# Gated linear attention with a mixer on one core: TensorE's small products in two groups a unit, with 48 weight columns for the later updates of the state

## The chip, the core and the metric

The kernel runs on one core of a Trainium2 chip. Its time is the device time of one execution in microseconds; the median of three runs is given. The core has a matrix engine (TensorE, PE in the profile, with its weight loads shown as PEld), a vector engine (VectorE, DVE), a scalar engine (ScalarE, ACT), GpSimd (POOL) and SyncE (SP), which here issues the transfers between memory and the core. Each engine works through its own queue in order, and they meet at semaphores.

## The reference

An attention with gates, in which each head keeps a 48 x 48 state that decays by a gate for every row, and then a mixer over the sequence and the channels:

```python
# q, k, v, f_logit: (4, 8, 768, 48)
f = 1.0 / (1.0 + np.exp(-f_logit))
for t in range(S):
    state = f[:, :, t, :, None] * state + einsum('bhd,bhe->bhde', k[:, :, t], v[:, :, t])
    y[:, :, t] = einsum('bhd,bhde->bhe', q[:, :, t], state)
x = y.transpose(0, 2, 1, 3).reshape(4, 768, 384)
# U: (768, 32), V: (32, 768), w_ch1: (384, 1536), w_ch2: (1536, 384)
u = x + (x.transpose(0, 2, 1) @ U @ V).transpose(0, 2, 1)
out = u + np.maximum(u @ w_ch1, 0.0) @ w_ch2
```

All arithmetic is in 32-bit floats.

## The kernel before

The attention is cut into 16 units, four for each batch; a unit is two heads of one batch. The two heads lie in the two halves of the 128 partitions, each padded from 48 to 64 rows (PAD). The 768 steps are cut into 12 chunks of 64. Within a chunk the products of gates are formed by scans on VectorE, the queries and keys are scaled by them, and what a chunk passes on is a 48 x 48 matrix.

A unit has a front, made by `prepare`, and a rear, made by `attend`. The front, mostly VectorE: `gates` (turn the gate logits, sigmoid on ScalarE), `keep` (backward scan L694), `keys` (turn and scale), `read_back` (forward scan L712), `queries` (turn and scale). Up to unit 5 the turning is done by TensorE's transposes (L660), later by VectorE (L637). The rear, mostly TensorE:

- `scores` (L788): keys times queries inside each chunk, 24 matmuls of 64 x 64, into the tile `sc`; VectorE masks it into `A` (L795).
- `kept` (L809): 12 transposes of the keys into `pt`, copied by ScalarE to `kb`.
- `states` (L825): `kb` times v, 24 matmuls into `ds`. The weights are 64 columns a head, of which 48 carry data. One ScalarE copy (L831) moves it to `added`.
- `scan` (L846): one VectorE scan runs the state through all chunks; after batch 0 ScalarE copies the result to `st` (L851).
- `read` (L863): queries times `st`, 22 matmuls that open the accumulation in `y`. A tiny ScalarE copy `seen` (L870) of one column follows.
- `inner` (L881): `A` times v, 24 matmuls that add to `y`; they wait for `seen`. ScalarE copies `y` to `x` (L887).

These matmuls fill only a quarter of TensorE's array each (64 rows by 64 columns; the key transposes half of it), and four of them can be in flight together. The matmuls of the mixer use the whole array: `pz` (L258, first layer, with a relu on ScalarE, L268), `po` (L283, second layer), `pw` (L312, second layer with seven products for eight), `pp` (L410, a scheme with fewer products for the last blocks), and the low-rank part (`ph`, `pu`, `put`).

The attention of a batch is interleaved with the mixer of the batch before. `steps(first, last)` yields the pieces of the attention, ten for a unit in the middle of a range; `attention` calls `Fill` before each piece, which hands out that much of the mixer's big products as falls to one piece. TensorE's order is the order in which the pieces are called. VectorE's and ScalarE's orders are also taken as called up to the attention of batch 1; later a scheduler sets them by priority. In step n, `steps` calls:

```python
for n in range(first, last):
    yield from rear(n - 1, "scores") + rear(n, "kept") + front(n + 1, "gates", "keep", "keys")
    yield from rear(n - 1, "read")
    made = rear(n, "states", "scan")
    yield lambda: [f() for f in made]
    yield from front(n + 1, "read_back", "queries") + rear(n - 1, "inner")
    if n + 2 < NU:
        load(n + 2, "v")
```

So big products can fall between any two of these. The outputs of all matmuls lie in PSUM: `ps_big` has three tiles of two banks for the small products, the transposes and some others, `ps_mm` two of one bank for `pz`, `po` and `pw`. v lies in three buffers, loaded by `load`.

Of the kernel before, what the change touches and what calls it, by code (L numbers as in the profile page):

```python
# [21 lines left out]
PAD = 64  # L22
# [450 lines left out]
def factored_path(ctx, tc, q, k, v, f_logit, moe_U, moe_V, moe_w_ch1, moe_w_ch2, out, ok):  # L473
# [4 lines left out]
    nc = tc.nc  # L478
    B, H, S, D = q.shape
    P = nc.NUM_PARTITIONS  # L480
# [3 lines left out]
    NBL = S // P  # L484
# [6 lines left out]
    NU = B * HP  # L491
# [36 lines left out]
    v_tiles = {}  # L528

    def load(n, *names):  # L530

        b, hp = divmod(n, HP)
        for nm in names:
            if nm == "v":
                v_tiles[n] = three.tile([P, NBL, 2, D], F32, name="v_nat")
            for par in range(2):
                head = src[nm][b, 2 * hp + par]
                if nm == "v" and par:

                    for s in range(2):  # L540
                        nc.sync.dma_start(
                            out=v_tiles[n][(1 - s) * C : (2 - s) * C, :, par, :],
                            in_=head.rearrange("(c s p) d -> s p c d", s=2, p=C)[s],
                        )
                    continue
                if nm == "v" or n < TURNED:
                    dst = v_tiles[n] if nm == "v" else nat[n % 2][nm]
                    nc.sync.dma_start(out=dst[:, :, par, 0:D], in_=head.rearrange("(c p) d -> p c d", p=P))
                    continue
                head = head.rearrange("(c i) d -> i c d", i=NB)  # L550
                for part in range(2):
                    p0 = par * PAD + part * NB
                    n_ch = min(NB, D - part * NB)
                    nc.sync.dma_start(  # L554
                        out=raw[n % 2][nm][p0 : p0 + NB, :].rearrange("p (c d) -> p c d", d=NB)[:, :, 0:n_ch],
                        in_=head[:, :, part * NB : part * NB + n_ch],
                    )
# [38 lines left out]
    added = const.tile([P, D * NCH + 1], F32, name="added")  # L596
# [173 lines left out]
    def attend(n):  # L770

        b, hp = divmod(n, HP)
        T = units[n]
        vt = v_tiles[n]
        rows = [slice(par * PAD, par * PAD + D) for par in range(2)]
        chunk = [slice(c * C, (c + 1) * C) for c in range(NCH)]

        part = [slice(s * C, (s + 1) * C) for s in range(2)]
# [37 lines left out]

        def states():

            ds = ps_big.tile([P, 2, 512], F32, name="ds", tag="big")
            for c in range(NBL):  # L820
                for s in range(2):
                    for par in range(2):

                        i = (c + (s & par)) % NBL
                        nc.tensor.matmul(  # L825
                            ds[par * PAD : (par + 1) * PAD, s, c * D : (c + 1) * D],
                            lhsT=T["kb"][part[s ^ par], par, i, :], rhs=vt[part[s ^ par], c, par, :],
                            start=True, stop=True,
                        )

            nc.scalar.copy(  # L831
                added[:, 1:].rearrange("p (e c s) -> p e c s", c=NBL, s=2),
                ds[:, :, 0 : NBL * D].rearrange("p s (c e) -> p e c s", e=D),
            )

        def scan():

            st = T["st"] = two.tile([P, NCH, D], F32, name="st")
            by_e = "p (e c) -> p c e"
            if b == 0:  # L840
                states = st.rearrange("p c e -> p (c e)")
                T["st"] = states.rearrange(by_e, c=NCH)
            else:
                states = added[:, 0 : D * NCH]
            with tc.high_priority(offset=AHEAD):
                nc.vector.tensor_tensor_scan(  # L846
                    states, added[:, 0 : D * NCH], T["whole"].rearrange("p e c -> p (e c)"), 0.0, ALU.add, ALU.mult
                )
                if b > 0:

                    nc.scalar.copy(st, states.rearrange(by_e, c=NCH))  # L851
# [20 lines left out]
        def inner():  # L872
# [18 lines left out]
            del units[n], v_tiles[n]  # L891

        return [kept, states, scan, scores, read, inner]

    ahead, here = {}, {}

    def front(n, *names):

        if n >= NU:
            return []  # L900
        if n not in ahead:
            ahead[n] = dict(zip(("gates", "keep", "keys", "read_back", "queries"), prepare(n)))
        return [ahead[n].pop(nm) for nm in names]

    def rear(n, *names):

        if not 0 <= n < NU:
            return []
        if n not in here:
            here[n] = dict(zip(("kept", "states", "scan", "scores", "read", "inner"), attend(n)))  # L910
        return [here[n].pop(nm) for nm in names if nm in here[n]]

    def steps(first, last):


        for n in range(first, last):
            yield from rear(n - 1, "scores") + rear(n, "kept") + front(n + 1, "gates", "keep", "keys")
            yield from rear(n - 1, "read")
            made = rear(n, "states", "scan")
            yield lambda: [f() for f in made]  # L920
            yield from front(n + 1, "read_back", "queries") + rear(n - 1, "inner")
            if n + 2 < NU:
                load(n + 2, "v")

    def attention(pieces, portions, todo):

# [28 lines left out]
    with tc.manual_schedule(engines={nc.vector.engine, nc.scalar.engine}):  # L955
# [53 lines left out]

        EARLY = 6  # L1010
        second = chain(front(HP, "gates", "keep", "keys", "read_back", "queries"), steps(HP, 2 * HP + 1))
        for i, (_, piece) in enumerate(start + m.firsts[1:]):
            piece()
# [6 lines left out]
        n = len(m.seconds) // (NBL // 2)  # L1020
# [6 lines left out]
    for b in range(2, B - 1):  # L1027
        todo, after = m.main, m.after
        attention(steps(b * HP + 1, (b + 1) * HP + 1), 10 * HP, todo)
        m = start_mixer(b, after)  # L1030

    pieces = beside(steps((B - 1) * HP + 1, NU + 1), 10 * (HP - 2), [lambda i=i: sum_of_w(i) for i in range(len(W_SUMS))])
    todo = m.first(0) + m.ready(0) + m.second(0)
    attention(pieces, 29, todo[:-1])
# [316 lines left out]
@with_exitstack  # L1351
def kernel(
    ctx: ExitStack,
    tc: tile.TileContext,
    q: bass.AP,
    k: bass.AP,
    v: bass.AP,
    f_logit: bass.AP,
    moe_U: bass.AP,
    moe_V: bass.AP,  # L1360
    moe_w_ch1: bass.AP,
    moe_w_ch2: bass.AP,
    out: bass.AP,
):


    nc = tc.nc
    args = (q, k, v, f_logit, moe_U, moe_V, moe_w_ch1, moe_w_ch2, out)
    flag = ctx.enter_context(tc.tile_pool(name="flag", bufs=1))
    ok = flag.tile([1, 1], I32, name="ok")  # L1370
    with ExitStack() as inner:
        factored_path(inner, tc, *args, ok)
    good = nc.values_load(ok[0:1, 0:1], min_val=0, max_val=1)
    with tc.If(good == 0):
        with ExitStack() as inner:
            general_path(inner, tc, *args)
# [30 lines left out]
```

## Time and profile before

| | |
|---|---|
| median of three runs | 488.37 us (487.12 to 489.71) |
| the profiled execution | 487.2 us |
| its span from first to last instruction | 485.4 us |
| VectorE busy | 356.6 us |
| ScalarE busy | 163.0 us |

The groups of instructions of the small products (line, engine, operation, output<-inputs, array rows*columns, shapes, count | busy us, mean ns of one), from the page and its longer list:

```profile
L863 PE MATMUL y<-st,qT 48*64 48x48 f32 x704 | 15.8, 232 | 0.2 <-DVE A L795 0.2
L881 PE MATMUL y<-v_nat,A 64*64 64x48 f32 x768 | 15.1, 221 | 3.4 <-issue 1.7 <-ACT seen L870 1.7
L825 PE MATMUL ds<-v_nat,kb 64*64 64x48 f32 x768 | 14.9, 220 | 0.0
L788 PE MATMUL sc<-qT,kz 48*64 48x64 f32 x768 | 14.8, 221 | 0.0
L825 PEld LDWEIGHTS ds<-v_nat,kb 64*64 64x64 f32 x768 | 13.3, 134 | 2.9 <-issue 2.4 <-ACT w_y L90 0.5
```

A matmul of 32-bit floats appears as two records, so 768 are 16 units of 24 matmuls. The mean of one (220 ns) is its latency; some 14.6 ns lie between one record and the next when 48 of them take 0.70 us. The busy time of a group is therefore far below count times mean. The idle time at the end of a line is that of the engine just before such instructions, with what ended it.

### The profile page before, as it was taken

The page shows a single profiled execution, that of the slowest core. Times are in us where ns is not written, and L with a number is a line of the kernel's source. Part 1 is how long each engine was busy: PE and PEld are TensorE (multiplying, and loading weights), DVE is VectorE, ACT ScalarE, POOL GpSimd, SP SyncE. Part 2 cuts the span into 40 slices and gives each one's busy share as a digit, 9 for nine tenths or more (in the row PEclk, how much of TensorE's full clock was granted, in tenths as well). Part 3 has the DMA queues.
Part 4 walks back from the last instruction along what each step waited for, and adds up shares of the span by engine and source line. Part 5 has one row for each costly group of instructions (what it writes and reads, how often), then busy time and mean ns, then how long its engine had stood idle before and what let it go on. Part 6 is the DMA issues. An engine that isn't in the chain of part 4 may idle for free.

```text
span 485.4 us, 12721 instructions
## 1 busy us (share of the span) xinstructions
PE 466.8 (96%) x5535; PEld 399.3 (82%) x5535; DVE 356.6 (73%) x563; ACT 163.0 (34%) x309; POOL 37.6 (8%) x49
## 2 busy tenths in 40 slices
PE   7996899999999999999999999999999999999995
PEld 4774788886566568899899888899979999999995
DVE  5888788877999757656857448797896886858642
ACT  2445566563344313424231403433231312112200
POOL 3001255443000000000000000000000000000000
PEclk9999999999999999999999999999999999999999
DMA  9989976666777522433535100100000000000001
GB/s 143 162 167 168 275 184 148 158 135 79 116 114 113 101 41 27 62 38 78 72 49 95 24 18 18 27 3 20 19 1 1 33 2 18 16 1 34 1 33 38
DMA packets 158679, 34.34 MB, mean 71 GB/s; under 512 B 149206, under 2 KB 157078, under 8 KB 158614
## 3 DMA queue, kind: packets, MB, share of 16 engines
q1 hardware_dynamic: 158614, 33.44, 37.6%
q8 instruction: 45, 0.74, 0.6%
q14 instruction: 20, 0.16, 0.1%
HBM read 28.70 MB, written 4.72 MB: 69 GB/s over the span
## 4 chain that ended last, share of the span: by engine, by line
PE 73%; DVE 13%; DMA 5%; SPq 3%; issue 3%; ACT 2%; POOL 0%; DVEq 0%
PE pw L312 26%; PE pz L258 19%; PE pp L410 11%; PE y L863 2%; PE pt L660 2%; PE y L881 2%; SPq L554 2%; PE ds L825 2%; DVE late L712 2%; DMA late<-in_f_logit_dram 2%; PE po L283 2%; DMA other<-in_f_logit_dram 2%; PE sc L788 1%; PE put L246 1%; DVE late L694 1%
## 5 line engine op out<-in xcount | busy, mean ns | idle before, releaser
L258 PE MATMUL pz<-uT,w 128*128 128x256 f32 x504 | 115.7, 384 | 0.3 <-ACT uT L247 0.3
L258 PEld LDWEIGHTS pz<-uT,w 128*128 128x128 f32 x504 | 93.6, 190 | 13.1 <-issue 0.5
L312 PE MATMUL pw<-w,z_all 128*128 128x192 f32 x216 | 37.7, 329 | 0.0
L312 PE MATMUL pw<-zw,w_raw 128*128 128x192 f32 x216 | 37.4, 328 | 0.0
L312 PEld LDWEIGHTS pw<-zw,w_raw 128*128 128x128 f32 x216 | 35.2, 190 | 0.8 <-issue 0.6
L312 PEld LDWEIGHTS pw<-w,z_all 128*128 128x128 f32 x216 | 35.0, 190 | 0.7
L95 POOL TENSOR_TENSOR w<-w_y,w_r 128x384 int32<-128x384 int32 x24 | 31.5, 1312 | 39.8 <-DVE w_y L94 34.4
L694 DVE TENSOR_TENSOR_SCAN late<-fz,late 128x768 f32<-128x768 f32 x16 | 28.1, 1755 | 8.8 <-ACT fz L689 4.2
L268 ACT ACTIVATE z_all<-pz 128x512 f32<-128x512 f32 x33 | 19.6, 595 | 39.6 <-PE pz L258 39.5
L410 PE MATMUL pp<-v_nat,late 128*128 128x128 f32 x224 | 28.8, 275 | 0.0
L712 DVE TENSOR_TENSOR_SCAN late<-fz,other 128x768 f32<-128x768 f32 x16 | 27.9, 1746 | 0.1
L410 PEld LDWEIGHTS pp<-v_nat,late 128*128 128x128 f32 x224 | 27.0, 192 | 0.0
L283 PE MATMUL po<-w,zw 128*128 128x384 f32 x72 | 25.6, 500 | 0.0
L283 PE MATMUL po<-w,z_all 128*128 128x384 f32 x72 | 25.3, 496 | 0.3 <-DVE o L187 0.3
L403 ACT ACTIVATE other<-other 128x512 f32<-128x512 f32 x18 | 11.3, 631 | 39.9 <-DVE other L187 39.9
L851 ACT COPY st<-added 128x576 f32<-128x576 f32 x12 | 14.7, 1224 | 27.5 <-DVE added L846 27.5
L92 DVE TENSOR_SCALAR w_y<-w_y 128x384 f32<-128x384 f32 (+3 forms) x27 | 12.8, 475 | 13.5 <-ACT w_y L90 13.3
L795 DVE TENSOR_TENSOR A<-sc,causal 128x768 f32<-128x768 f32 x16 | 15.2, 948 | 9.9 <-PE sc L788 9.9
L283 PEld LDWEIGHTS po<-w,z_all 128*128 128x128 f32 x72 | 13.1, 190 | 8.7 <-DVE o L187 0.9
L283 PEld LDWEIGHTS po<-w,zw 128*128 128x128 f32 x72 | 13.0, 190 | 8.7 <-issue 1.2
L881 PEld LDWEIGHTS y<-v_nat,A 64*64 64x64 f32 x768 | 13.1, 134 | 8.5 <-issue 5.1
L187 DVE TENSOR_TENSOR w_raw<-z_all 128x768 f32<-128x768 f32 x12 | 11.5, 955 | 10.5 <-ACT z_all L268 9.2
(193 smaller groups left out, 829.9 us busy)
## 6 DMA issues: line engine op xcount, KB each, us to landing
w_raw<-in_moe_w_ch_dram SPq DMA_DIRECT2D x18, 384.0 KB, 3.9
out_dram<-o SPq DMA_DIRECT2D x24, 192.0 KB, 1.9
v_nat<-in_v_dram SPq DMA_DIRECT2D x16, 144.0 KB, 3.2
v_nat<-in_v_dram SPq DMA_DIRECT2D x32, 72.0 KB, 3.5
zw<-in_moe_w_ch_dram SPq DMA_DIRECT2D x6, 384.0 KB, 4.2
late<-in_f_logit_dram SPq DMA_DIRECT2D x10, 96.0 KB, 3.0
late<-in_k_dram SPq DMA_DIRECT2D x10, 96.0 KB, 2.7
late<-in_q_dram SPq DMA_DIRECT2D x10, 96.0 KB, 2.6
```

Of the source, the lines that this page charges most:

```text
L92: nc.vector.tensor_scalar(f, f, SMALLEST, LARGEST, ALU.max, ALU.min)
L95: nc.gpsimd.tensor_tensor(dst.bitcast(I32), shaped(y.bitcast(I32)), shaped(r), ALU.add)
L258: nc.tensor.matmul(pm[:, i * 2 * P : (i + 1) * 2 * P], lhsT=w1[:, m, o : o + P], rhs=uT[a][:, m, :], start=(m == 0), stop=(m == NDC - 1))
L268: nc.scalar.activation(z[a, c][:, k : k + 2, :].rearrange("p i t -> p (i t)"), pm, AF.Relu)
L283: nc.tensor.matmul(pm, lhsT=z[a, i // NI][:, i % NI, s * P : (s + 1) * P], rhs=w2[:, i, :], start=(i == 0), stop=(i == NFC - 1))
L312: nc.tensor.matmul(pm[:, n * HM : (n + 1) * HM], lhsT=lhs[:, i, :], rhs=rhs[:, i, :], start=(i == 0), stop=(i == NI - 1))
L410: nc.tensor.matmul(pm[:, i, r * P : (r + 1) * P], lhsT=room["w"](wn)[:, r * P : (r + 1) * P], rhs=x_node(a, xn), start=((xn, wn) == of[0]) ...
L694: nc.vector.tensor_tensor_scan(backwards(X, S - 1, S), backwards(f, S, S), backwards(ends, S - 1, S), 0.0, ALU.mult, ALU.add,)
L712: nc.vector.tensor_tensor_scan(Y, f[:, 0:S], starts, 0.0, ALU.mult, ALU.add)
L795: nc.vector.tensor_tensor(T["A"], sc[:, :, 0 : NBL * C].rearrange("p h (c i) -> p h c i", i=C), causal.unsqueeze(1).unsqueeze(1).broadcast ...
L851: nc.scalar.copy(st, states.rearrange(by_e, c=NCH))
L881: nc.tensor.matmul(o(s, par, c), lhsT=T["A"][part[s ^ par], par, c, :], rhs=vt[part[s ^ par], c, par, :], start=False, stop=True, skip_gro ...
```

## The change

`steps` joins pieces. `joined` takes several lists, yields an empty piece for each but one of those that hold anything, and then one piece that calls all of them in a row; so the number of pieces, and with it the share of big products, stays nearly the same. In step n the inner products of unit n-2, the scores of unit n-1 and the key transposes of unit n stand together, and the read of unit n-1 together with the update of the state of unit n. The inner products of a unit come one step after its read, except at the end of a range, where they follow at once. v of unit n+1 is loaded in step n behind the first group, in place of v of unit n+2 at the end of step n. From batch 1 on (`if b`), the update takes 48 columns of `kb` as weights and writes 48 of the 64 rows of each half of `ds`; ScalarE copies the two halves of 48 rows each, one after the other.

```diff
         def states():
 
+            M = D if b else PAD
             ds = ps_big.tile([P, 2, 512], F32, name="ds", tag="big")
...
                         nc.tensor.matmul(
-                            ds[par * PAD : (par + 1) * PAD, s, c * D : (c + 1) * D],
-                            lhsT=T["kb"][part[s ^ par], par, i, :], rhs=vt[part[s ^ par], c, par, :],
+                            ds[par * PAD : par * PAD + M, s, c * D : (c + 1) * D],
+                            lhsT=T["kb"][part[s ^ par], par, i, 0:M], rhs=vt[part[s ^ par], c, par, :],
                             start=True, stop=True,
                         )
 
-            nc.scalar.copy(
-                added[:, 1:].rearrange("p (e c s) -> p e c s", c=NBL, s=2),
-                ds[:, :, 0 : NBL * D].rearrange("p s (c e) -> p e c s", e=D),
-            )
+            for r in rows if b else [slice(0, P)]:
+                nc.scalar.copy(
+                    added[r, 1:].rearrange("p (e c s) -> p e c s", c=NBL, s=2),
+                    ds[r, :, 0 : NBL * D].rearrange("p s (c e) -> p e c s", e=D),
+                )
...
+    def joined(*groups):
+
+        groups = [g for g in groups if g]
+        for _ in groups[1:]:
+            yield lambda: None
+        if groups:
+            yield lambda: [f() for g in groups for f in g]
+
     def steps(first, last):
 
-
         for n in range(first, last):
-            yield from rear(n - 1, "scores") + rear(n, "kept") + front(n + 1, "gates", "keep", "keys")
-            yield from rear(n - 1, "read")
-            made = rear(n, "states", "scan")
-            yield lambda: [f() for f in made]
-            yield from front(n + 1, "read_back", "queries") + rear(n - 1, "inner")
-            if n + 2 < NU:
-                load(n + 2, "v")
+            yield from joined(rear(n - 2, "inner"), rear(n - 1, "scores"), rear(n, "kept"))
+            if n + 1 < NU and n + 1 not in v_tiles:
+                load(n + 1, "v")
+            yield from front(n + 1, "gates", "keep", "keys")
+            yield from joined(rear(n - 1, "read"), rear(n, "states", "scan"))
+            yield from front(n + 1, "read_back", "queries")
+            if n + 1 == last:
+                yield from rear(n - 1, "inner")
+                if n + 2 < NU:
+                    load(n + 2, "v")
```

## The prediction

> **What bounds the kernel now.** I read the page, then the chain of waits in order of time, then TensorE's own waits, then busy time by stage, and last the timelines of VectorE and ScalarE where the chain leaves TensorE.
>
> ```profile
> PE 466.8 (96%) x5535; PEld 399.3 (82%) x5535; DVE 356.6 (73%) x563; ACT 163.0 (34%) x309; POOL 37.6 (8%) x49
> ```
>
> TensorE is busy for 466.8 of 485.4 us, so time that leaves TensorE counts, unless another engine is as full in the same stage. Busy time by stage (columns: TensorE, its weight loads, VectorE, ScalarE):
>
> ```profile
> 120.00:134.00 14.00, 13.37 (x230) 8.24 (x229) 12.96 (x16) 5.31 (x10) 0.00 (x0) 1.00 0.76 114
> 134.00:145.00 11.00, 11.00 (x188) 7.14 (x187) 9.96 (x13) 4.28 (x9) 0.00 (x0) 1.00 0.72 113
> 205.00:230.00 25.00, 25.00 (x370) 22.98 (x367) 15.50 (x23) 8.12 (x16) 0.00 (x0) 1.00 0.39 63
> 292.00:314.00 22.00, 22.00 (x364) 18.39 (x364) 17.62 (x23) 8.88 (x16) 0.00 (x0) 1.00 0.08 16
> ```
>
> In the attention of batches 2 and 3 (about 182 to 335 us) TensorE is full and VectorE is not. In batch 1 (up to 168 us) both are full. There VectorE's timeline has one idle gap of 0.90 us a unit, always for the sigmoid of the gates, and no other wait:
>
> ```profile
> 140.08 1.76 DVE L694 TENSOR_TENSOR_SCAN late<-fz,late 128x768 f32<-128x768 f32 x1 [0.90 <-ACT fz L689]
> 152.13 1.76 DVE L694 TENSOR_TENSOR_SCAN late<-fz,late 128x768 f32<-128x768 f32 x1 [0.90 <-ACT fz L689]
> ...
> 165.58 1.76 DVE L712 TENSOR_TENSOR_SCAN late<-fz,other 128x768 f32<-128x768 f32 x1
> 167.25 0.53 DVE L187 TENSOR_TENSOR o<-x,po 128x384 f32<-128x384 f32 x1
> ```
>
> ```profile
> 167.83 4.14 PE L283 MATMUL po<-w,z_all 128*128 128x384 f32 x12 [0.27 <-DVE o L187]
> ```
>
> A unit takes VectorE 12.05 us (140.08 to 152.13), and it runs so from 115.4 to 167.8; TensorE then waits for its addition at 167.25. That stage is VectorE's.
>
> The price of a small group is in the chain (start, length, instructions; a float matmul is two records, so x48 is 24 matmuls):
>
> ```profile
> 177.53 1.96 PE put L246 x18
> 179.49 2.59 PE pz L258 x12
> 182.09 0.86 PE sc L788 x48
> ...
> 191.43 0.83 PE y L863 x44
> 192.26 2.79 PE pz L258 x12
> 195.05 0.84 PE ds L825 x48
> ...
> 217.07 0.77 PE y L863 x42
> 217.90 0.70 PE ds L825 x46
> ```
>
> After big matmuls x48 takes 0.84; after another small group 0.70. The twelve big ones behind a small group take 2.79, otherwise 2.59. An excursion into small tiles thus costs 0.14 + 0.20 = 0.34 us beyond its matmuls. The transposes of the keys (L809) take 0.52 either way, so joining a lone one saves only the 0.20.
>
> **What the Trainium skill says.** "TensorEngine Tiling (Array Packing)", Key Properties: changing the tiling mode drains TensorE. The trace agrees: 0.34 us. "TensorE: Matmul & The Clock Gate", LDWEIGHTS: the load's time goes with the columns of the weights, not the rows. The trace agrees: 190 ns for 128 columns, 134 to 135 for 64, with 48 rows as with 64. The same page's table of specifications: ScalarE and VectorE are strict first-in-first-out. The trace agrees: at 130 us the small copy `seen` stood behind ScalarE's L699, which waited for VectorE, and TensorE's inner products waited 0.63 us for it.
>
> **The change part by part.** The order of the built programs shows how many excursions there are from unit 4's update of the state on.
>
> *Joining.* Batch 1: 16 runs of small products become 10; batch 2: 16 become 9; batch 3: 9 become 7. In batch 2, five of the seven joins save 0.34 and two are lone key transposes at 0.20: 2.1 us. In batch 3, one of each: 0.54 us. In batch 1, three of each: 1.6 us, but behind VectorE.
>
> *48 weight columns.* Twelve units' updates load 48 columns, not 64. From 190 and 134 ns a column costs 56/64 = 0.875 ns, so 16 columns are 14 ns; four tiles load side by side, 48 passes are 12 turns: 0.17 us a unit. It is nothing if the moving side sets the pace, but L788 moves 64 columns and L825 48, and both take 0.70 to 0.71 for x48; so the weights do, or the issue. I take 0.16: four units in batch 2 0.64, three in batch 3 0.48. Bounds 0 and 0.17 a unit.
>
> *Two copies.* ScalarE copies `ds` in two halves of 48 partitions with the same 576 elements each; L831's row has 641 ns, so the second costs 0.64 (bounds 0.32, if partitions counted, and 0.64). ScalarE is a third busy. Behind the copies stand the scan L846 and the copy to `st`. In batch 1 the first copy ended at 118.0, 130.65, 142.7 and 155.2, and L846 began at 120.1, 132.1, 144.15 and 156.2: at least 1.0 us of cover, so it costs nothing; without cover up to 0.64 a unit.
>
> *Inner products a step later.* This removes the waits for `seen` at 117 and 130 us (0.29 and 0.63), both in batch 1. The last unit's 0.26 stays, since there reading and inner products still follow each other. The output bank of `y` is held longer, but the built program lets the key transposes wait for the bank of `ds`, long free. The v loads are issued a step later, still some 10 us ahead of use, and SP's queue order hardly moves.
>
> *Batch 1 as a whole.* TensorE could give up 1.6 + 5 x 0.16 + 0.92 = 3.3 us. VectorE's order there is the same instruction for instruction, apart from places of one product mask; its 52 us stay, and TensorE waits at 167 us. What is left is how much earlier VectorE starts: one join of 0.20 and one update of 0.16 lie before 110 us, 0.3 us after rounding down. So 3.0 us are hidden.
>
> *A new wait.* In batches 2 and 3 the read and the update now stand together. VectorE's queries wait for the read (here 2.85 us), then scan L712, then scan L846, then ScalarE's `st`, and only behind it in ScalarE's order the relu that frees a bank of `pz`:
>
> ```profile
> 192.31 0.98 DVE L637 STREAM_TRANSPOSE qT<-late 128x768 f32<-128x768 f32 x1 [2.85 <-PE y L863]
> ...
> 196.69 1.36 DVE L846 TENSOR_TENSOR_SCAN added<-added,whole 128x576 f32<-128x576 f32 x1 [0.61 <-ACT added L831]
> ```
> ```profile
> 198.08 1.22 ACT L851 COPY st<-added 128x576 f32<-128x576 f32 x1 [1.42 <-DVE added L846]
> ```
>
> From the end of the read to the end of that relu: 1.0 + 1.0 + 1.7 + 1.35 + 1.15 + 0.55 = 6.75 us. Before, 3.6 us of `pz` and the update lay between read and update; now, for unit 9, TensorE has 0.55 (update) + 0.25 + 2 x 2.59 = 6.0 us of work until its third `pz` needs that bank. I take 0.8 us for unit 9 and 0.1 for unit 12, where inner products fill the gap; the other five have a longer product there, or the relu ahead of `st`. Bounds 0 and 0.8 for each of the seven: 0 to 5.6.
>
> **Sum.** Batch 1 -0.3; batch 2 -2.1 -0.64 +0.9 = -1.84; batch 3 -0.54 -0.48 = -1.0. Together -3.1 us. The profiled execution took 487.2 us (span 485.4, 1.8 around it), so 484.1 on its own terms. It is 1.2 below the median of the three runs, 488.37; against that I forecast 485.3, 0.6% less.
>
> **Rivals.**
> (a) *The whole saving arrives*: VectorE yields in batch 1 and no new wait appears. For it: VectorE's gaps for the sigmoid (0.9 a unit) could fill with other work. Against it: the same order. 3.3 + 2.74 + 1.02 = 7.1, so 481.3.
> (b) *No change that can be measured*: the narrow weights bring nothing (+1.1), and new waits take one more microsecond. For it: pairs of loads and matmuls may be issue-bound. Against it: pauses of the weight loads inside these groups. About 487.4.
> (c) *Slower*: the relu behind `st` becomes a TensorE wait in every unit of batches 2 and 3. At 0.9 us a unit over seven units (6.3) it beats the 3.95 gained by more than 0.5%; at 1.0 it gives 7.0 - 3.95 = +3.0, 491.4. For it: ScalarE's extra 0.64 and in-order queue, no cover known from the trace. Against it: TensorE has no wait at all between 168 and 333 us, and only unit 9 has three `pz` behind the pair.
>
> **How the numbers follow.** Chances: forecast 0.50 (its own range 483.8 to 486.8), (a) 0.13, (b) 0.26, (c) 0.11. The range takes in (a) and (b): 481.3 to 488.8, leaving out (c) and edges. A measurement of this kernel can tell 0.5%, 2.4 us, from no change. Below 485.9 lie (a) and 0.36 of the forecast's 0.50: faster 0.49. Same: the rest of it and (b), 0.40. Slower: 0.11.
>
> **What would show it.** In the profile after: fewer small runs, each entry still 0.14 and return 0.20; L826 x48 near 0.54 instead of 0.70 (right about weights) or still 0.70; TensorE waits of some 3 us in all before 168 us, at the key transposes or the addition `o`; VectorE's unit still 12.05 us; one wait of 0.8 us at a `pz` near 205 us. I am wrong if TensorE doesn't wait in batch 1, if the scan period there grows past 12.1 (the second copy lost its cover), or if waits for the relu recur in most units.

## The result, and the profile after

The changed kernel takes 485.70 us (median of 19 runs, 484.98 to 488.29), the kernel before 488.14 (19 runs beside them, 487.12 to 492.39). The ratio is 0.9952, with a 95% interval from 0.9939 to 0.9966: 0.5% faster. The forecast was 485.3.

The profiled execution took 486.3 us, with a span of 484.5. Its busy times, from the page:

```profile
PE 463.1 (96%) x5535; PEld 397.8 (82%) x5535; DVE 358.2 (74%) x563; ACT 170.7 (35%) x321; POOL 37.7 (8%) x49
```

TensorE is busy 3.7 us less than before, with the same instructions; VectorE 1.6 and ScalarE 7.7 us more (12 copies more, of about 0.64 us each). The span fell by 0.9 us only. The rest is waiting, and a slower start.

**The start.** Busy time of the profiled execution after in one stretch of it; the third figure from the end is the granted clock:

```profile
52.90:56.10 3.20, 3.20 (x12) 2.77 (x11) 0.00 (x0) 0.80 (x1) 0.00 (x0) 0.50 1.11 225
```

Between about 52.8 and 56.2 us TensorE ran at half speed, and at full speed in the stretches on both sides (49 to 52.8 and 56.3 to 60 us). In the profiled execution of before no such stretch is seen (mean clock 1.00). The first instruction of TensorE that the change touches is unit 4's update of the state (`ds`), and up to it the two kernels give every engine the same instructions in the same order; it starts 90.10 us after the first matmul before and 91.69 after, 1.59 later. Half speed for 3.4 us can lose up to 1.7 us, but how much of the 1.59 it lost stays open: three executions of the experiments below, all with the new order and without a half-speed stretch in the start, took 90.21, 90.27 and 91.60 us for the same instructions. In all the profiled executions the start takes from 90.10 to 91.94 us with the old order and from 90.21 to 92.39 with the new one in batch 1. So these 1.6 us are put down to the execution and not to the change, and stages have to be compared by themselves.

**The stages.** I cut the trace at matmuls that both kernels have: the first of unit 4's update (`ds`), the `put` of batch 1 (177.37 us before), the next `put`, the first `lp` and the last matmul. Start to start, in us; the experiments below are in the same table:

| kernel | `ds` of unit 4 to `put` (batch 1) | `put` to `put` (batch 2) | `put` to `lp` (batch 3) | `lp` to the last |
|---|---|---|---|---|
| before | 84.52 | 112.43 | 44.57 | 145.29 |
| after | 84.23 | 111.28 | 43.56 | 145.29 |
| joins only | 84.34 | 111.37 | 44.03 | 145.29 |
| columns only | 84.53 | 111.79 | 44.09 | 145.29 |
| joins in batch 1 only | 84.34 | 112.43 | 44.57 | 145.29 |
| joins after batch 1 only | 84.52 | 111.49 | 44.04 | 145.29 |
| before, lighter VectorE | 83.57 | 112.43 | 44.57 | 145.28 |
| after, lighter VectorE | 81.05 | 111.27 | 43.56 | 145.29 |
| after, `st` on VectorE | 84.92 | 111.44 | 43.56 | 145.28 |
| both of these | 81.06 | 111.43 | 43.56 | 145.28 |
| joins and second copy | 84.36 | 111.56 | 44.03 | 145.28 |
| one copy of 112 rows | 84.34 | 111.17 | 43.80 | 145.28 |
| the same, lighter VectorE | 81.45 | 111.16 | 43.81 | 145.28 |

A stage that a kernel does not change repeats within 0.02 us from one execution to the next (last column, or batch 2 of three kernels at 112.43), so a tenth of a microsecond can be read here, though the whole time scatters by 2 us. From before to after the change gives -0.29, -1.15 and -1.01, together -2.45; with the 1.59 of the start that is -0.86, the fall of the span.

**Batch 1 after.** Busy time by stage, shifted by the 1.3 us by which this execution is late there (columns as before: TensorE, weight loads, VectorE, ScalarE):

```profile
121.30:135.30 14.00, 13.53 (x271) 9.10 (x262) 12.96 (x16) 6.05 (x11) 0.00 (x0) 1.00 0.75 112
135.30:146.30 11.00, 10.76 (x121) 6.40 (x119) 9.96 (x13) 4.99 (x10) 0.00 (x0) 1.00 0.77 120
```

VectorE's 12.96 and 9.96 us are those of before to the hundredth; TensorE, which was full in the second of the two (11.00 of 11), now has a gap there, and in the first another than before. VectorE's backward scans:

```profile
129.31 1.76 DVE L694 TENSOR_TENSOR_SCAN late<-fz,late 128x768 f32<-128x768 f32 x1 [0.90 <-ACT fz L689]
...
141.36 1.76 DVE L694 TENSOR_TENSOR_SCAN late<-fz,late 128x768 f32<-128x768 f32 x1 [0.90 <-ACT fz L689]
```

The period is still 12.05 us. All of TensorE's labelled waits between 115 and 240 us, from its timeline:

```profile
127.63 0.76 PE L826 MATMUL ds<-v_nat,kb 64*48 64x48 f32 x48 [0.47 <-issue]
...
139.68 0.76 PE L826 MATMUL ds<-v_nat,kb 64*48 64x48 f32 x48 [0.24 <-issue]
...
161.39 1.48 PE L172 MATMUL ph<-x,U 128*32 128x384 f32 x12 [0.39 <-ACT x L889]
...
169.13 4.14 PE L283 MATMUL po<-w,z_all 128*128 128x384 f32 x12 [1.18 <-DVE o L187]
...
203.12 5.45 PE L258 MATMUL pz<-uT,w 128*128 128x256 f32 x24 [1.06 <-ACT z_all L268]
```

The two waits for `seen` of before are gone. In their place TensorE waits 0.47 + 0.24 + 0.39 + 1.18 = 2.3 us before 170 us, and there is one new wait at 203 us. ("issue" means that the profile shows nothing that ended the wait.)

**Batch 2 after.** The chain of waits in order of time:

```profile
196.19 0.99 DVE qT L637
197.21 0.97 DVE qT L675
198.20 1.76 DVE late L712
199.96 1.26 DVE added L848
201.24 1.21 ACT st L853
202.47 0.61 ACT z_all L268
203.12 5.45 PE pz L258 x24
208.57 0.84 PE y L883 x48
209.41 0.71 PE sc L788 x48
210.13 0.51 PE pt L809 x12
```

The last three lines are a joined group: the first x48 pays the entry (0.84), the second does not (0.71). The lines ahead of them are the new wait: from the end of the read VectorE turns and scales the queries, makes two scans, ScalarE copies `st`, and only then makes the relu whose bank `pz` needs. That is the chain of the forecast, link by link.

### The profile page after: what moved, and what is told of

The parts are those of the page before. It is cut to its first block, busy times and chain, and to the rows that moved or that the text cites. A ratio compares the mean times of both kernels' runs of the same rounds, so it can differ in the third digit from the quotient of the medians.

```text
span 484.5 us, 12730 instructions
## 1 busy us (share of the span) xinstructions
PE 463.1 (96%) x5535; PEld 397.8 (82%) x5535; DVE 358.2 (74%) x563; ACT 170.7 (35%) x321; POOL 37.7 (8%) x49
## 4 chain that ended last, share of the span: by engine, by line
PE 69%; DVE 16%; DMA 6%; ACT 3%; SPq 3%; issue 3%; POOL 0%; DVEq 0%; POOLq 0%; ACTq 0%
PE pw L312 26%; PE pz L258 17%; PE pp L410 11%; DVE late L712 2%; PE y L865 2%; DVE late L694 2%; PE y L883 2%; DMA late<-in_f_logit_dram 2%; PE pt L660 2%; PE po L283 2%; SPq L548 2%; PE sc L788 1%; DVE added L848 1%; DVE w_y L94 1%; PE put L246 1%
## 5 line engine op out<-in xcount | busy, mean ns | idle before, releaser
L258 PEld LDWEIGHTS pz<-uT,w 128*128 128x128 f32 x504 | 94.6, 192 | 15.5 <-ACT z_all L268 1.5
L833 ACT COPY added<-ds 48x576 f32<-48x576 f32 (+1 forms) x28 | 17.8, 636 | 4.2 <-PE ds L826 3.8
L403 ACT ACTIVATE z_all<-z_all 128x512 f32<-128x512 f32 x12 | 7.6, 630 | 32.8 <-DVE z_all L187 32.8
```

Of the source, the lines that this page charges most:

```text
L258: nc.tensor.matmul(pm[:, i * 2 * P : (i + 1) * 2 * P], lhsT=w1[:, m, o : o + P], rhs=uT[a][:, m, :], start=(m == 0), stop=(m == NDC - 1))
L403: nc.scalar.activation(dst, dst, AF.Relu, scale=float(SIGNS[n]))
L833: nc.scalar.copy(added[r, 1:].rearrange("p (e c s) -> p e c s", c=NBL, s=2), ds[r, :, 0 : NBL * D].rearrange("p s (c e) -> p e c s", e=D),)
```

## The experiments

Eleven kernels. Each was timed against the kernel before, whose medians beside them were 488.58 us (the first four kernels), 488.67 (the next four) and 488.30 (the last three); the profiled execution gave the stages of the table.

**Joins only.** The new order of the pieces, with 64 columns and one copy everywhere.

```diff
-            M = D if b else PAD
+            M = PAD
-            for r in rows if b else [slice(0, P)]:
+            for r in [slice(0, P)]:
```

> The two groups a unit, with 64 weight columns and one copy of ds as before. My theory (TensorE counts after batch 1, VectorE binds batch 1): the 48 columns give 0.16 us for each of the seven updates after 168 us and nothing before, so without them the changed kernel's gain of 2.4 us falls by about 1.1 to 1.3 us below the kernel before; x48 of the update takes 0.70 us again. Rival (the narrow weights bring nothing, all is the joining): 2.4 us as in the whole change.

Measured: 486.50 us, ratio 0.9953 (0.9938 to 0.9969). That is 2.1 us below the kernel before and not the 1.1 to 1.3 expected; by the whole time alone the rival's 2.4 could not be ruled out. By stage the joins alone bring 0.18, 1.06 and 0.54 us. Batch 3 is the forecast's 0.54, and batch 1 its 0.20 for the one join before VectorE binds. But the whole change is only 0.11 + 0.09 + 0.47 = 0.67 us better than this, of which 0.09 in batch 2, where the narrow weights should have been worth 0.64. So the two parts do not add up in batch 2; the runs further down say why.

**Columns only.** The order of before, with 48 columns and two copies from batch 1 on (shown against the kernel after).

```diff
-            yield from joined(rear(n - 2, "inner"), rear(n - 1, "scores"), rear(n, "kept"))
...
+            yield from rear(n - 1, "scores") + rear(n, "kept") + front(n + 1, "gates", "keep", "keys")
+            yield from rear(n - 1, "read")
+            made = rear(n, "states", "scan")
+            yield lambda: [f() for f in made]
+            yield from front(n + 1, "read_back", "queries") + rear(n - 1, "inner")
```

> 48 weight columns and two copies alone, in the old order of the pieces. My theory: seven updates of 0.16 us, 1.1 us below the kernel before, x48 of the update about 0.54 us beside another small group and 0.68 us behind big products; TensorE waits more before 168 us by what it saves there. Rival (the second copy on ScalarE costs): no gain or slower, with new waits at the scan of the state or at a relu.

Measured: 487.11 us, ratio 0.9971 (0.9959 to 0.9984). Batch 2 gains 0.64 and batch 3 0.48, which is four and three units at 0.16 us exactly; laid side by side with the trace of before, batch 2 steps ahead by 0.16 at each of the four updates and nowhere else. In batch 1 it gains nothing: its waits for `seen` grow from 0.29 and 0.63 us to 0.61 and 0.79, and that for `o` from 0.27 to 0.59.

The group of these weight loads in the kernel after (mean ns of one behind the comma) shows the term itself; 64 columns took 134 before:

```profile
L826 PEld LDWEIGHTS ds<-v_nat,kb 64*48 64x48 f32 x576 | 8.5, 121 | 1.2 <-issue 1.2
```

13 ns for 16 columns, against the 14 of the forecast. In the traces the loads of unit 9's update start in fours within 20 ns: from one four to the next it is 55 to 59 ns before and 42 to 45 here. But with 48 columns the matmuls of the update shorten as well, from 220 to 207 ns each (L825 before, L826 after), so these runs do not separate the weight load from the matmul; they show that the number of columns counts.

**Joins in batch 1 only, and joins after batch 1 only** (64 columns, one copy). `steps_joined` is the new `steps`, `steps` that of before; only the calls that change are shown.

```diff
-steps(HP, 2 * HP + 1)
+steps_joined(HP, 2 * HP + 1)
```

```diff
-steps(b * HP + 1, (b + 1) * HP + 1)
+steps_joined(b * HP + 1, (b + 1) * HP + 1)
-steps((B - 1) * HP + 1, NU + 1)
+steps_joined((B - 1) * HP + 1, NU + 1)
```

> The joined order only while the units of batch 1 run, 64 columns, one copy. My theory: VectorE's 12.05 us a unit set that stage, so the 1.6 us of fewer changes of tiling and the 0.9 us of waits for the small copy turn into TensorE waits before 169 us; 0 to 0.3 us below the kernel before. Rival (TensorE counts there too): 2.5 us below.

> The joined order only for the units of batches 2 and 3, 64 columns, one copy. My theory: 2.1 + 0.54 us saved, about 1.1 us lost in one wait for a relu behind the copy to st: 1.2 to 1.6 us below the kernel before, and this with the run that joins in batch 1 only adds up to the run with all joins. Rival (the gain comes from batch 1): no change.

Measured: in batch 1 only 488.35 us, ratio 0.9990 (0.9968 to 1.0012), which is no change that can be told; after batch 1 only 486.98, ratio 0.9961 (0.9947 to 0.9975). By stage the first gains 0.18 in batch 1 and nothing later, the second nothing in batch 1, then 0.94 and 0.53. Together that is 1.65, against 1.78 with all joins; most of the 0.13 that are missing lies in batch 2. TensorE's waits between 100 and 200 us with joins in batch 1 only:

```profile
128.45 0.92 PE L826 MATMUL ds<-v_nat,kb 64*64 64x48 f32 x48 [0.47 <-issue]
...
167.84 0.91 PE L180 MATMUL ph<-h,blocks 128*128 128x384 f32 x2 [0.22 <-ACT h L175]
...
169.93 4.14 PE L283 MATMUL po<-w,z_all 128*128 128x384 f32 x12 [1.18 <-DVE o L187]
```

The time the joins free there comes back as waits, above all for VectorE's addition `o`. The joins that pay are those of batches 2 and 3.

**A lighter VectorE, before and after.** If VectorE hides batch 1's gain, taking work off it must let the gain through. The product of the queries (L675) of units up to 9 goes to GpSimd, which is idle there.

```diff
-                nc.vector.tensor_tensor(t, t, T[of], ALU.mult)
+                on = nc.gpsimd if nm == "q" and n <= 2 * HP + 1 else nc.vector
+                on.tensor_tensor(t, t, T[of], ALU.mult)
```

> The kernel before, with the product that scales the queries of units 6 to 9 moved from VectorE (0.96 us each) to GpSimd, which is idle there. My theory: in the kernel before TensorE is full in batch 1 too, so only its waits there can go (0.9 for the small copy, 0.3 for the addition): 0 to 1.2 us below the kernel before; VectorE's unit falls from 12.05 towards 11.1 us plus new waits. Rival (GpSimd and VectorE hinder each other, so VectorE's other instructions grow): slower than before.

> The changed kernel with the same four products on GpSimd. My theory: the 3 us that VectorE held back in batch 1 come free, as far as 4 x 0.96 us reach: 2.3 to 3 us below the changed kernel, 4.7 to 5.4 us below the kernel before, and TensorE's waits before 169 us nearly gone. Rival (something other than VectorE's time holds batch 1, the transfers or ScalarE): no more than 1 us below the changed kernel.

Measured: before with this edit 487.91 us, ratio 0.9982 (0.9967 to 0.9996); after with it 483.48 us (6 runs), ratio 0.9905 (0.9876 to 0.9934), 2.2 us below the whole change, just short of the 2.3 to 3 expected. The same edit brings 0.95 us in batch 1 to the kernel before and 3.18 us to the kernel after. All labelled waits of TensorE from 60 to 340 us that are left in the latter:

```profile
61.38 5.45 PE L258 MATMUL pz<-uT,w 128*128 128x256 f32 x24 [0.28 <-ACT uT L247]
...
199.58 5.45 PE L258 MATMUL pz<-uT,w 128*128 128x256 f32 x24 [1.06 <-ACT z_all L268]
...
329.11 0.92 PE L884 MATMUL y<-v_nat,A 64*64 64x48 f32 x48 [0.26 <-ACT seen L873]
```

No wait is left in batch 1, and its busy time by stage reads (the fifth engine is GpSimd):

```profile
121.30:135.30 14.00, 14.00 (x246) 9.34 (x243) 13.00 (x15) 7.44 (x13) 1.82 (x1) 1.00 0.73 111
135.30:146.30 11.00, 11.00 (x213) 7.08 (x211) 10.00 (x13) 5.31 (x10) 1.81 (x1) 1.00 0.81 126
```

TensorE is full again, and VectorE's unit is 11.03 us (its backward scans start at 127.89 and 138.92 us). From before to here batch 1 falls by 84.52 - 81.05 = 3.47 us. The forecast put what TensorE could give up there at 3.3 us, and 0.27 for `o` was waited for already: 3.57. So all but 0.1 of the saving is there, and in the kernel after VectorE hid all but 0.3 of it.

**`st` copied by VectorE.** The new wait at 203 us stands behind the copy to `st` on ScalarE. VectorE makes it from batch 2 on.

```diff
-                    nc.scalar.copy(st, states.rearrange(by_e, c=NCH))
+                    copy = nc.vector.tensor_copy if b > 1 else nc.scalar.copy
+                    copy(st, states.rearrange(by_e, c=NCH))
```

> The changed kernel with the copy to st done by VectorE for the units of batches 2 and 3. My theory: the relu no longer stands behind that copy on ScalarE, so TensorE's wait of 1.06 us at a pz near 203 us goes, and VectorE has room there: 0.8 to 1.3 us below the changed kernel. Rival (the wait has another cause, or VectorE's extra copies delay additions): no gain, the wait stays or others appear.

Measured: 486.86 us, ratio 0.9965 (0.9951 to 0.9979), no gain on the whole change, where 0.8 to 1.3 us were expected. TensorE's timeline, and VectorE's copy of unit 8:

```profile
201.86 5.45 PE L258 MATMUL pz<-uT,w 128*128 128x256 f32 x24 [0.52 <-ACT z_all L268]
...
225.53 2.83 PE L258 MATMUL pz<-uT,w 128*128 128x256 f32 x12 [0.73 <-DVE w_y L187]
```

```profile
157.41 0.68 DVE L854 COPY st<-added 128x576 f32<-128x576 f32 x1
```

The wait at 203 us halves, from 1.06 to 0.52. So the copy to `st` is one cause of it, and not the only one. ScalarE's timeline shows what is left: another copy, to `whole` (L815), waits for the same scan and now stands ahead of the relu.

```profile
200.51 0.67 ACT L815 COPY whole<-whole 128x576 f32<-128x576 f32 x1 [3.13 <-DVE added L848]
201.21 1.09 ACT L268 ACTIVATE z_all<-pz 128x512 f32<-128x512 f32 x2
```

And two things take the gain back. The copy, 0.68 us, now stands in VectorE's order ahead of the additions `o` and `w_y`, which a `pz` near 226 us waits for. And unit 8, whose batch is 2, has its update still inside the stage of batch 1: there VectorE sets the pace, and the stage grows from 84.23 to 84.92, by 0.69 us, the length of the copy.

**Both.** The last two edits together.

> Both: four products on GpSimd and the copy to st on VectorE after batch 1. My theory: the two gains are in different stages and add up: 3.1 to 4.3 us below the changed kernel, about 6 us below the kernel before. Rival (one hides the other): no more than the better of the two.

Measured: 483.90 us, ratio 0.9907 (0.9877 to 0.9937), as with the lighter VectorE alone and not the sum that was expected. Batch 1 is at 81.06: with VectorE no longer the bound, the same 0.68 us copy of unit 8 costs nothing.

**The second copy only.** Why do the columns bring 0.09 us in batch 2 beside the joins, and 0.64 without them? First suspect: the second copy of `ds`, which stands ahead of the relu in ScalarE's order. Joins and two copies, 64 columns:

```diff
-            M = D if b else PAD
+            M = PAD
```

> The joins and the two copies of ds, but all updates with 64 weight columns. Theory (the second copy is what eats most of the columns' gain in batch 2, because it lengthens the way to the relu that the third pz of unit 9 waits for): against the joins alone the wait at that pz grows from 0.78 to about 1.05 us, the stage of batch 2 from 111.4 to 111.7 or more, the stage of batch 3 stays at 44.0, and the time is about 487.0, 0.3 to 0.5 above the joins alone. Rival (the columns are worth little once the groups are joined, and the copy costs nothing): the wait stays at 0.78, the stage of batch 2 at 111.4.

**One copy of 112 rows.** The first head's update keeps 64 columns, the second head's takes 48, so that a single copy covers both.

```diff
-            M = D if b else PAD
+            M = [PAD, D if b else PAD]
...
-                            ds[par * PAD : par * PAD + M, s, c * D : (c + 1) * D],
-                            lhsT=T["kb"][part[s ^ par], par, i, 0:M], rhs=vt[part[s ^ par], c, par, :],
+                            ds[par * PAD : par * PAD + M[par], s, c * D : (c + 1) * D],
+                            lhsT=T["kb"][part[s ^ par], par, i, 0 : M[par]], rhs=vt[part[s ^ par], c, par, :],
...
-            for r in rows if b else [slice(0, P)]:
+            for r in [slice(0, PAD + M[1])]:
```

> The whole change, but the first head's update keeps 64 columns and only the second head's takes 48, so that one ScalarE copy of 112 partitions does. Theory (second copy): the wait at the pz of unit 9 falls from 1.06 to about 0.78 plus whatever the earlier update adds, the stage of batch 2 from 111.28 to about 111.0, and batch 3 lies between 43.56 and 44.03 if the weights of the two heads load in turn (about 43.8), or at 44.03 if the wider one sets the pace. Time some 0.2 below the whole change to equal. Rival (the copy costs nothing): batch 2 at 111.3 or above, time 0.2 to 0.5 above the whole change.

Measured: the second copy only 486.86 us, ratio 0.9969 (0.9958 to 0.9980); one copy 485.95, ratio 0.9957 (0.9938 to 0.9977). The times alone tell little between them; the stages and one place do. With the second copy only batch 2 is at 111.56 instead of 111.37, 0.19 more, where 0.3 or more was expected; the wait at the third `pz` of unit 9 is 0.90 us, where 1.05 was expected. The timelines about it, first joins only (one copy), then after (two copies):

```profile
197.44 0.64 ACT L833 COPY added<-ds 128x576 f32<-128x576 f32 x1 [0.62 <-PE ds L826]
...
200.34 1.33 DVE L848 TENSOR_TENSOR_SCAN added<-added,whole 128x576 f32<-128x576 f32 x1
201.71 1.21 ACT L853 COPY st<-added 128x576 f32<-128x576 f32 x1 [3.63 <-DVE added L848]
202.82 0.59 ACT L268 ACTIVATE z_all<-pz 128x512 f32<-128x512 f32 x1
...
203.47 3.72 PE L258 MATMUL pz<-uT,w 128*128 128x256 f32 x16 [0.78 <-ACT z_all L268]
```

```profile
196.81 1.28 ACT L833 COPY added<-ds 48x576 f32<-48x576 f32 x2 [0.46 <-PE ds L826]
...
199.88 1.33 DVE L848 TENSOR_TENSOR_SCAN added<-added,whole 128x576 f32<-128x576 f32 x1
201.24 1.21 ACT L853 COPY st<-added 128x576 f32<-128x576 f32 x1 [3.15 <-DVE added L848]
202.47 0.60 ACT L268 ACTIVATE z_all<-pz 128x512 f32<-128x512 f32 x1
...
203.12 4.15 PE L258 MATMUL pz<-uT,w 128*128 128x256 f32 x18 [1.06 <-ACT z_all L268]
```

After, the two copies end at 196.81 + 1.28 = 198.09 us, and the scan that reads them starts at 199.88, behind VectorE's own queue. There are 1.8 us of room, so the copies are not on the path, and neither is the update of the state. My suspicion was wrong in its main part. Two small terms are left:

- The path runs from the end of the read over VectorE and ScalarE to the relu, and does not contain the update, which TensorE does meanwhile. Narrow weights let TensorE arrive 0.16 us earlier and wait 0.16 us longer.
- With two copies the relu starts 202.47 - 201.24 = 1.23 us behind the start of the copy to `st`, with one copy 1.11 (202.82 - 201.71). The second copy only shows 1.23 too, and one copy of 112 rows 1.12, so these 0.12 us go with the number of copies. With one copy the relu starts 0.10 us before the copy to `st` has ended, with two 0.02 after it. Why, these runs do not show.

So the wait of the whole change is 0.78 + 0.16 + 0.12 = 1.06. The other versions agree: two copies alone 0.78 + 0.12 = 0.90, as measured; the mixed one, with half of the columns' gain and one copy, 0.78 + 0.08 = 0.86, and 0.85 in its trace. Its batch 2 is 111.17, and batch 3 is 43.80, halfway between 64 and 48 columns.

The same happens a second time at a `pz` near 226 us, whose bank VectorE's addition `w_y` frees. First joins only, then after:

```profile
224.46 2.11 PE L312 MATMUL pw<-w,w_raw 128*128 128x192 f32 x12
...
225.79 0.35 DVE L187 TENSOR_TENSOR w_y<-w_y,pw 128x192 f32<-128x192 f32 x1
...
226.41 2.75 PE L258 MATMUL pz<-uT,w 128*128 128x256 f32 x12
```

```profile
223.94 2.11 PE L312 MATMUL pw<-w,w_raw 128*128 128x192 f32 x12
...
225.57 0.35 DVE L187 TENSOR_TENSOR w_y<-w_y,pw 128x192 f32<-128x192 f32 x1
...
226.06 2.83 PE L258 MATMUL pz<-uT,w 128*128 128x256 f32 x12
```

With joins only, `pz` starts 1.95 us behind the last `pw`, the distance that two runs of twelve `pw` have there; `w_y` is no hindrance. After, it starts 2.12 us behind, just after `w_y` has ended at 225.92. TensorE came 0.16 us earlier and VectorE did not. The timeline of after has no label for so short a wait; that of the version with `st` on VectorE, where it is 0.73, names `w_y`.

Laid side by side, after steps ahead of the second copy only by 0.16 us at each of the four updates of batch 2, and falls back by 0.16 at these two `pz`: of 0.64 us 0.32 are left by this count, and 0.28 by the stages (111.56 - 111.28).

**One copy, and the lighter VectorE.**

> As the one before, and the queries' product of units 6 to 9 on GpSimd. Theory (VectorE hides batch 1, the second copy costs 0.3 in batch 2): no wait of TensorE between 61 and 199 us, a pz wait of about 0.8 there, time 483.3, equal to or up to 0.4 below the version with the lighter VectorE and two copies. Rival: equal to that version or above it, since the narrower weights of one head are lost in every unit.

Measured: 482.91 us (5 runs), ratio 0.9893 (0.9865 to 0.9921). The wait at `pz` is 0.85, and no other is labelled between 61 and 199 us, as expected. The interval overlaps that of the lighter VectorE with two copies (483.48), and the sum of the stages is 0.5 us higher (81.45 + 111.16 + 43.81 against 81.05 + 111.27 + 43.56), since the narrow columns of one head are lost; the lower median is then not shown to be a gain. Both beat before and after by at least 2 us.

## Why the prediction was right

**Batch 1, -0.3: right, -0.29.** VectorE's unit stayed at 12.05 us, TensorE's saving turned into waits, and what is left is the one join and the one update ahead of it. The lighter VectorE freed 3.18 us after the change; the forecast had 3.0 hidden. The waits were put at some 3 us. By the stage they are 84.23 - 81.05 = 3.2 us against the version in which none is left; the labelled ones sum to 2.3, and where the other 0.9 are is not shown. They were forecast at the key transposes or at `o`: 1.18 are at `o`, 0.39 at `ph`, and the 0.71 ahead of the update have no releaser in the profile.

**Joins, 0.34 for an excursion and 0.20 for a lone transpose: right.** Batch 3 alone: 0.54 expected, 0.54 measured. In batch 2 the 2.1 are seen only together with the new wait: joins only gave 1.06.

**48 columns, 0.16 a unit: right.** Measured 0.64 in batch 2 by themselves, 0.48 in batch 3. The rival that they bring nothing is gone. That it is the weight load which sets the pace fits, since the loads got as much shorter, but the matmuls did too.

**Two copies, nothing in batch 1: right** (84.36 with the second copy only, 84.34 with joins only), and by the trace for its reason, the room ahead of the scan L848, which is 1.8 us in unit 9 too. Not foreseen are the 0.12 us at the relu, and 0.07 us inside the run of twelve `pz` at 226 us (2.83 us after and with the second copy only, 2.75 with joins only).

**The new wait, 0.9: at unit 9 the right place and chain, and too small.** This is the term that was mis-sized. Its first part, 0.8 at unit 9's third `pz`, is 1.06 us by the label in the trace after. Start to start it is more. The place after:

```profile
195.87 0.24 PE L826 MATMUL ds<-v_nat,kb 64*48 64x48 f32 x2
...
196.61 5.45 PE L258 MATMUL pz<-uT,w 128*128 128x256 f32 x24
```

The third `pz` starts at 203.12, so the 24 records take 6.51 us. Before, 24 behind a small group take 5.28 where no wait is labelled (from 93.69 us to the transposes at 98.97): a wait of 1.23 us. The forecast took the wait as the difference of two sums, 6.75 us for the chain and 6.0 for TensorE's work. Counted from the start of VectorE's queries (196.19), the chain is 203.12 - 196.19 = 6.93 us; 0.12 of the excess is the later relu. TensorE's work from there is 0.42 us to the first `pz` and 5.28, together 5.70. The forecast had counted the update in full, 0.55, but it begins at 195.87, while the last matmuls of the read still run; and it took 5.43 for the two runs of `pz`.

The second part, 0.1 at unit 12, did not come: behind that update, at 265 us, `pz` and the inner products run on without a labelled wait. Instead 0.16 us are lost at 226 us, behind unit 10's update, at a `pz` that waits for VectorE's addition and not for the relu. There the sum overlooked that the narrow weights' gain cannot arrive where a path beside the update ends later: of the 0.64 counted in full, 0.16 is waited away. At unit 9 the narrow update was already in the forecast's 6.0. Batch 2 with the measured terms: -2.1 - 0.64 + 1.23 + 0.16 + 0.07 = -1.28, against -1.15 measured and -1.84 forecast; 0.13 stay open.

**Batch 3, -1.0: right, -1.01**, 0.54 and 0.47.

**The sum.** The stages give -2.45 where -3.1 was forecast; the difference is batch 2. The medians differ by 2.44 us (488.14 and 485.70). That the median came within 0.4 us of 485.3 is in part luck: the gain was 0.65 smaller than forecast, and the kernel before was 0.23 faster in the 19 runs than in the three that the forecast started from. Of the rivals, the whole saving did not arrive because VectorE did not yield; no change was wrong because the narrow columns count, though its other half, larger new waits, came to 0.56 us (1.23 + 0.16 + 0.07 against 0.9); slower was wrong because the relu holds up one unit, not seven. Two slips in its figures change nothing: the gains that (c) sets at 3.95 add up to 4.06 (0.3 + 2.74 + 1.02), and 6.3 - 3.95 = 2.35 us is 0.48%, not more than 0.5%; and of the weight loads with 64 columns and 48 rows those of L863 take 138 ns, not 134 to 135.

The forecast for the profiled execution, 484.1, missed its 486.3 by 2.2: 1.6 are the later start, 0.7 is batch 2. The kernel before had been profiled in an execution without a half-speed stretch in the start, 0.9 us below its own median of the 19 runs. Its executions beside the experiments fit that: those with a mean clock of 0.998 or more have a median of 487.8 us (32), those with 0.993 or less 488.8 us (76).

## What to carry to other kernels

Grouping small matmuls paid here only in the stages where TensorE is the bound; in a stage where another engine is equally full, lighten that engine first (here one product of 0.96 us a unit on an idle engine), and the grouping's gain comes through. Putting two groups together also takes away the work that lay between them: list the chain that starts at the end of the first group, and compare it with the work TensorE has until it needs that chain's result. Two gains do not add where one of them shortens work that lies beside such a chain; there the shorter work only makes the wait longer.

## What the runs showed of the hardware

- A stretch at half clock comes in the start of some executions and not of others: 3.4 us long from 52.8 us (after), 6.8 us long from 50.8 us (joins only), none before. The start up to unit 4's update took from 90.10 us (before) to 92.39 us (joins in batch 1 only) with the same instructions; 91.60 is found without such a stretch too. Stages cut out of the trace behind it repeat within 0.02 us.
- A ScalarE copy of 48 partitions with 576 elements each takes as long as one of 112 or 128: 635 ns on average after, 641 ns for both others.
- GpSimd's product of 128 x 768 takes 1.82 us where VectorE takes 0.96, yet moving four of them there shortened the stage of the kernel after by 3.18 us, of the 3.8 us (4 x 0.96) that left VectorE. VectorE's masking beside the first three of them takes 0.94 us each, against 0.95 in the kernel after; the scan that begins beside the end of the fourth takes 1.84 against 1.76.
